# Attention and MLP block on one core: order of two VectorE reads in each attention slot, MLP factors in six pieces, and a rearranged opening

## The chip, the cores and the metric

The kernel runs on one NeuronCore of a Trainium2 chip. The metric is the device time of one execution in microseconds (us). The five engines are TensorE (PE, with its weight loads as PEld), VectorE (DVE), ScalarE (ACT), GpSimd (POOL) and SyncE (SP), which issues most of the DMAs. Each works through its own list of instructions in order and waits on semaphores.

## What is computed

The reference is one transformer block with 2048 rows of 576 values. Attention has 32 query heads of 128 on 16 key and value heads, over the last 512 entries of a cache; the MLP has 4608 hidden columns.

```python
mod = silu(c) @ w_mod                 # six vectors: sa, ca, ga, sb, cb, gb
h = layernorm(x) * (1 + ca) + sa
q = h @ wq                            # 32 heads of 128
p = softmax(q @ k.T * 128 ** -0.5)    # k, v: the last 512 rows, one pair for 2 query heads
x = x + ga * (concat(p @ v) @ wo)
h = layernorm(x) * (1 + cb) + sb
x = x + gb * ((silu(h @ w1) * (h @ w3)) @ w2)
```

## The kernel before

**Halves.** fp32 operands of a product are split into an fp16 high part and an fp16 remainder, the low part, after a scaling by a power of two. A product is then three products of halves: high by high, high by low, low by high. High parts are casts on ScalarE or GpSimd. Low parts are subtractions on GpSimd, or one instruction on VectorE.

**Slots and steps.** The rows are four blocks of 512 (`b`), each four tiles of 128 (`t`). Attention is a list of 128 slots `i`, one for each pair of a head and a block, and a slot has four steps `t` = 0 to 3, one for each row tile. The loop at L1564 writes out the order by hand, and each engine keeps it. Tasks that prepare later slots hang on a table: `at(i, t, task)` puts a task behind step `t` of slot `i`, and `step_at` counts steps of four to a slot. In step `t` of slot `i`:

- `scores(i, t)` (L475): three PE products into one of two banks `pss`. DVE takes the row maximum (L487) and makes the exponent's offset (L488).
- `weights` (L491): ACT's exponential `p` (L500) reads that bank and frees it. `half_high` and `half_low` split `p` on ACT and POOL, and a transposing DMA turns three of the four tiles. The fourth is turned on PE at `t` = 1 of the next slot: ACT casts it (L527), and DVE makes its low part (`turn_low`, L552, `ptw`) at `t` = 2.
- `query(i + 1, t)` (L410, L414): a part of the next slot's query product, for `t` < 3. ACT writes the high part of `qT` (L467), DVE the low part (L473).
- `attend_out` (L584): half of the product of one row tile with `wo`, six PE matmuls into the two banks `pe` (L433). There is one buffer `pe`. Every second call ends a tile, at `t` = 1 and at `t` = 3, and DVE then adds the tile into the accumulator (L592, `acc<-pe,factors,acc`). The next call's matmuls must wait until that read of `pe` is over.
- `normalize(i - 2)` (L567) at `t` = 1: DVE multiplies the value product `po` of an earlier slot with the softmax denominators `r`, which a DMA spreads over the partitions, into `on` (L571). `split_on` splits `on` at `t` = 3.
- At the end of a slot, `values(i - 1)` (L554): twelve PE products with `v` into `po` (L562). The third needs the low part of `ptw`, so L552.

Before the change the `normalize` call stands ahead of `attend_out` in step `t` = 1, right behind the score product.

**Opening.** Before slot 0, the first block goes through layernorm statistics on DVE (`norm_stats`, `bn_stats` and `bn_aggr`), modulation vectors, and `modulate_first`, which makes `h` of block 0 in halves. `put_in` splits a head's `wq` (`split_in`: two passes on ACT, then POOL's subtraction). `scale_first` finds one scale for the modulation vectors: a maximum, a small PE product, and a chain of small DVE instructions. Statistics of block 1 run on DVE behind `modulate_first`: two tiles ahead of slot 0's low part of `qT`, two behind it. `h` of block 1 is needed by the query product of slot 2, which is spread over slot 1. For each of its five column groups `m`, `make_h` has PE transpose four tiles into one of two banks `pt` (L240), DVE or ACT read the bank into `hf` (L249, L251), POOL cast that to the high part (L252) and POOL subtract for the low part (L254, L256). The values `v` of group 0 are peaked (`find`), scaled and split (L376 on ACT, L367 on DVE) by tasks in slots 0 and 1.

**MLP factors.** `act_factors` (L1180) makes a table of factors on DVE in five pieces, hung on five steps near the end of attention and, for the second half of the table, on five steps of the MLP.

Of the kernel before, what the change touches and what calls it, by code (L numbers as in the profile page):

```python
# [20 lines left out]
P = 128  # L21
# [27 lines left out]
def tile_block(  # L49
# [140 lines left out]
    def norm_stats(b, t):  # L190
# [4 lines left out]
            nc.vector.bn_stats(st[:, h, :], acc[b][:, t, h * HALF : (h + 1) * HALF])  # L195
        nc.vector.bn_aggr(norms[b][0][:, t, :], st.rearrange("p a b -> p (a b)"))

    def norm_root(b):
        rstd = norms[b][0][:, :, 1]
        nc.vector.tensor_scalar(rstd, rstd, EPS, None, op0=ALU.add)  # L200
        nc.scalar.activation(rstd, rstd, AF.Sqrt)

    def norm_scale(b):
# [15 lines left out]
    def norm_rows(b, t):  # L219

        mv, xn = norms[b]
        xt = pool.tile([P, D + DR], F32, tag="xn", name="xn", bufs=ST)
        if t < 2 or b not in shifts:
            nc.vector.tensor_scalar(
                xt[:, :D], acc[b][:, t, :], mv[:, t, 0:1], mv[:, t, 1:2], op0=ALU.subtract, op1=ALU.mult
            )
        else:
            nc.scalar.activation(
                xt[:, :D], acc[b][:, t, :], AF.Identity, bias=shifts[b][:, t : t + 1], scale=mv[:, t, 1:2]
            )  # L230
            if t == ST - 1:
                del shifts[b]
        nc.gpsimd.tensor_copy(xt[:, D:], xt[:, DC * P : D])
        xn[t] = xt

    def turn_rows(b, m, tag):

        ps = t_bank() if tag == "T" else bank(tag, "ps_n")
        for t in range(ST):
            nc.tensor.transpose(ps[:, t * P : (t + 1) * P], norms[b][1][t][:, m * P : (m + 1) * P], ident)  # L240
        return ps

    def modulate(hT, m, ps, shift, gain, on_vector=False):

        g, s = gain[:, m : m + 1], shift[:, m : m + 1]
        hf = pool.tile([P, SB], F32, tag="hf", name="hf", bufs=HF)
        high = hT[:, m if m < DC else 2 * DC, :]
        if on_vector:
            nc.vector.tensor_scalar(hf, ps, g, s, op0=ALU.mult, op1=ALU.add)  # L249
        else:  # L250
            nc.scalar.activation(hf, ps, AF.Identity, bias=s, scale=g)  # L251
        nc.gpsimd.tensor_copy(high, hf)  # L252
        if m < DC:
            nc.gpsimd.tensor_sub(hT[:, DC + m, :], hf, high)  # L254
        else:
            nc.gpsimd.tensor_sub(high[DR:], hf[DR:], high[DR:])  # L256

    def modulate_first(hT, turned, shift, gain):

        def make(m, h):  # L260
            g, s = gain[:, m : m + 1], shift[:, m : m + 1]
            if m % 2:
                nc.vector.tensor_scalar(h, turned[m], g, s, op0=ALU.mult, op1=ALU.add)
            else:
                nc.scalar.activation(h, turned[m], AF.Identity, bias=s, scale=g)

        for m in range(DC + 1):
            make(m, hT[:, m if m < DC else 2 * DC, :])
        for m in (DC, 1, 0, 3, 2):
            tag, bufs = ("p", PB) if m < DC else ("hf", HF)  # L270
            h = pool.tile([P, SB], F32, tag=tag, name="hf", bufs=bufs)
            make(m, h)
            if m < DC:
                (nc.vector if m % 2 else nc.gpsimd).tensor_sub(hT[:, DC + m, :], h, hT[:, m, :])
            else:
                nc.gpsimd.tensor_sub(hT[DR:, 2 * DC, :], h[DR:], hT[DR:, 2 * DC, :])

# [57 lines left out]
    def up_of(g, k):  # L335
        return peaks[g][:, 10 + k : 11 + k]

    def split_in(raw, g, j):

        w = pool.tile([P, 2, DC + 1, P], F16, tag="w", name="wq", bufs=WB)  # L340
        nc.scalar.activation(raw, raw, AF.Copy, scale=up_of(g, j))
        nc.scalar.copy(w[:, 0], raw)
        nc.gpsimd.tensor_sub(w[:, 1], raw, w[:, 0])
        return w

    def load_out(g):

# [735 lines left out]
    def scale_first(ps):  # L1083

        small = odd.tile([P, 16], F32, tag="us", name="us")
        nc.vector.tensor_scalar(mod_a[:, 1], mod_a[:, 1], 1.0, None, op0=ALU.add)
        nc.vector.tensor_reduce(small[:, 0:1], mod_a, axis=AX.XY, op=ALU.max, apply_absolute_value=True)
        spread = pool.tile([P, SB], F32, tag="kv", name="spread", bufs=8)
        nc.vector.tensor_scalar(spread[:, :P], ident, small[:, 0:1], None, op0=ALU.mult)
        nc.tensor.matmul(ps[:, :P], ones, spread[:, :P], start=True, stop=True)  # L1090
        nc.vector.tensor_reduce(small[:, 2:3], ps[:, :P], axis=AX.X, op=ALU.max)
        powers(small, small[:, 2:3], 0, 1, 5, 2.0**-9)
        nc.vector.tensor_scalar(mod_a, mod_a, small[:, 10:11], None, op0=ALU.mult)
        vecs["shift", "a"], vecs["gain", "a"] = mod_a[:, 0], mod_a[:, 1]
        nc.vector.tensor_scalar(score_down, small[:, 5:6], SCALE / Q_DOWN, None, op0=ALU.mult)

    def scale_gate(kind, small, to):

# [81 lines left out]
    def act_factors(lo, hi, piece):  # L1180

        top, h_down = mlp_small[:, 2:3], mlp_small[:, 5:6]
        both = stats.rearrange("p (g j) k -> p g j k", j=2)[:, lo:hi]
        downs, pairs = both[:, :, :, 0], both[:, :, :, 1]
        a = acts_down[:, lo:hi]
        if piece == 0:
            nc.vector.tensor_max(a, pairs[:, :, 0], pairs[:, :, 1])
            nc.vector.tensor_scalar(a, a, top, 2.5 * D * 2.0**-13.5, op0=ALU.mult, op1=ALU.mult)
        elif piece == 1:
            nc.vector.tensor_scalar(a, a, top, 2.0**-60, op0=ALU.mult, op1=ALU.max)  # L1190
            d = in_down[:, 2 * lo : 2 * hi]
            nc.vector.tensor_scalar(d, d, h_down, None, op0=ALU.mult)
        elif piece < 4:
            j = piece - 2
            nc.vector.reciprocal(pairs[:, :, j], a)
            nc.vector.tensor_mul(pairs[:, :, j], pairs[:, :, j], downs[:, :, j])
        else:
            if hi == G:
                hi += 1
                nc.vector.tensor_copy(acts_down[:, G : G + 1], acts_down[:, G - 1 : G])  # L1200
            d = out_down[:, lo:hi]
            nc.vector.tensor_scalar(d, d, mlp_gate_down, None, op0=ALU.mult)
            nc.vector.tensor_mul(d, d, acts_down[:, lo:hi])

    def find(into, u, k, *key):
# [56 lines left out]
    for u, (g, blocks, whole) in enumerate(uses):  # L1262
# [8 lines left out]
        if u:  # L1271
            A = dict(load=-22, keys=-17, wq=-13, total=-9, scale=-9, put=-8, turn=-5, vals=-1)
            if u == 1:
                A.update(load=-16, keys=-13, wq=-13)
            A = {k: R + v for k, v in A.items()}
            step_at(A["load"], load, keys, u, load_kv, k_cache, g)
            for j in range(2):
# [64 lines left out]
    for late in range(turns):  # L1342
# [15 lines left out]
            plan += [(step, make, number + k, maker, w, k), (step + STORE, store_now, number + k)]  # L1358
        for step, task, *args in plan:
            late_at(total + step, task, *args)  # L1360
    for piece in range(5):
        late_at(2 * len(ORDER) * turns + len(ORDER) + 1 + piece, act_factors, (NF - FEW) // 2, G, piece)
    for k, (i, t) in enumerate(((n - 4, 0), (n - 4, 2), (n - 3, 0), (n - 2, 0))):
        at(i, t, load_wset, 0, k)
# [36 lines left out]
    def begin_h(b):  # L1401
        hT[b] = new_h()

    def make_h(b, m, on_vector=False):
        modulate(hT[b], m, turn_rows(b, m, "T"), vecs["shift", "a"], vecs["gain", "a"], on_vector)

    def statistics(i, b, steps):
        for t in range(ST):
# [86 lines left out]
    at(109, 2, make_cols, "gain", "b", 4, 1.0, "T")  # L1495
    at(109, 3, lambda: spread_peaks("b", mlp_small))
    at(110, 1, lambda: scale_cols("b", t_bank(), mlp_small, 2.0**-8))
    for piece in range(5):
        step_at(ST * (n - 4) + 2 + piece, act_factors, 0, (NF - FEW) // 2, piece)
    for b in (2, 3):  # L1500
        for t in range(ST):
# [27 lines left out]
    warm(junk, WARM[0])  # L1529
    take_sums(0, 0, 3)  # L1530
    powers(peaks[0], peaks[0][:, 5:10], 0, 3, 5, 2.0**-14)
    put_in(0, 0)
    for m in (0, 1, 2, 3, 4):
        weigh_col(wms[1], 1, m, True)
    keys[0] = split_k(keys[0], 0)
    put_in(0, 1)
    scale_first(junk)
    warm(junk, WARM[1])
    begin_h(0)
    modulate_first(hT[0], turned, vecs["shift", "a"], vecs["gain", "a"])  # L1540
    score_factors(0)
    keys[0] = split_k_low(*keys[0], 0)
    for t in (0, 1):
        norm_stats(1, t)
    query(0, len(QP) - 1)
    for t in (2, 3):
        norm_stats(1, t)
    norm_root(1)
    at(0, 0, norm_scale, 1)
    at(0, 1, find, vals, 0, 3)  # L1550
    step_sum(3, totals, taken, 0, 3, 4)
    at(0, 3, find_scales, 0, 3, 4)
    at(1, -1, put_values, 0)
    at(1, 0, put_values_low, 0)
    for t in range(ST):
        at(0, t // 2, norm_rows, 1, t)
    at(0, 2, begin_h, 1)
    for m in range(DC + 1):
        at(*((0, 2), (0, 3), (1, -1), (1, 0), (1, 1))[m], make_h, 1, m, m % 2 == 1)
    for d, step in enumerate((5, 6, 7, 4, 5)):  # L1560
        step_at(step, weigh, 2, d)

# [1 line left out]
    for i in range(n + 2):  # L1564
        run(i, -1)
        for t in range(ST):
# [6 lines left out]
                turn(slot, tile)  # L1573
            if i < n:
                scores(i, t)
            if 2 <= i <= n and t == 1:
                normalize(i - 2)
            if 1 <= i <= n and t == 2:
                turn_low(i - 1, ST - 1)
                if i == n:  # L1580
# [20 lines left out]
                    next(stream)  # L1601
            for piece in outs.get((i, t), ()):
                attend_out(*piece, (i, ("total", t)))
            run(i, ("total", t))
            run(i, ("taken", t))
            run(i, t)
# [81 lines left out]
```

## Time and profile before

| | |
|---|---|
| median of 3 runs | 2758.36 us (2758.09 to 2758.54) |
| the profiled execution: time | 2758.39 us |
| the profiled execution: span in the trace | 2756.2 us |
| TensorE busy | 2685.1 us, 97% |
| VectorE, GpSimd, ScalarE busy | 72%, 68%, 59% |
| granted TensorE clock, mean | 0.995 |

The span reaches from the first to the last instruction of the trace; the execution's own time is 2.2 us longer. In the rows of a timeline the columns are start and duration in us, engine, line, operation, output<-inputs, shapes and count, and in brackets the idle time of that engine ahead of the row and what ended it. Rows of PE overlap by their pipeline's depth. In the rows of waits the three numbers are us in total, times, and the longest. Attention ends at about 1625 us; the rest is the MLP.

### The profile page before, as it was taken

How to read it: one execution, taken by the hardware profiler on the slowest of the kernel's cores; microseconds unless marked ns; L12 is line 12 of the kernel's file. 1: busy time of each engine (PE TensorE's matmuls, PEld its weight loads, DVE VectorE, ACT ScalarE, POOL GpSimd, SP SyncE). 2: the span in 40 equal slices, each digit the busy share in tenths (PEclk: the TensorE clock that was granted, in tenths of full speed). 3: DMA queues.
4: the chain of work that ended last, by engine and by line, in shares of the span. 5: the costliest groups of instructions: out<-in, count | busy, mean ns of one | idle time of the engine just before them, and what ended most of it. 6: DMA issues, size and time to landing. Idle time of an engine off the chain costs nothing. (4 is left out here: it accounts for less than half of the span.)

```text
span 2756.2 us, 44751 instructions
## 1 busy us (share of the span) xinstructions
PE 2685.1 (97%) x15406; PEld 1512.8 (55%) x15406; DVE 1997.3 (72%) x3555; ACT 1617.8 (59%) x3013; POOL 1881.1 (68%) x1748
## 2 busy tenths in 40 slices
PE   6899999999999999999999999999999999999998
PEld 3455555555555555555555555555555555555555
DVE  7877788877788787877876667777766656666666
ACT  5777778777777877777677735544443333333332
POOL 5577788888788977877669637688873465333435
PEclk8999999999999999999999999999999999999999
DMA  5778888778786887989889945656643444333332
GB/s 186 171 178 193 194 182 188 175 176 189 169 185 166 190 196 180 214 181 210 192 189 208 256 131 171 200 167 200 210 149 108 161 121 128 103 102 111 104 107 87
DMA packets 593460, 463.84 MB, mean 168 GB/s; under 512 B 442704, under 2 KB 472528, under 8 KB 592208
## 3 DMA queue, kind: packets, MB, share of 16 engines
q1 hardware_dynamic: 592944, 460.69, 65.5%
q8 instruction: 121, 1.98, 0.3%
q14 instruction: 107, 0.88, 0.1%
q10 hardware_dynamic: 288, 0.30, 0.0%
HBM read 264.19 MB, written 95.99 MB: 131 GB/s over the span
## 5 line engine op out<-in xcount | busy, mean ns | idle before, releaser
L537 POOL TENSOR_TENSOR hp<-p,hp 128x512 f16<-128x512 f32 x384 | 449.6, 1173 | 266.3 <-ACT hp L532 143.8
L500 ACT ACTIVATE p<-pss,table,factors 128x512 f32<-128x512 f32 x512 | 396.9, 775 | 354.9 <-DVE table L488 182.5
L849 PEld LDWEIGHTS <-wset 128*128 128x128 f16 x3528 | 344.5, 98 | 337.4 <-issue 4.4
L487 DVE TENSOR_REDUCE table<-pss 128x1 f32<-128x512 f32 x512 | 350.5, 685 | 206.0 <-PE pss L483 202.0
L849 PE MATMUL py<-hset,wset 128*128 128x512 f16 x2016 | 483.1, 380 | 0.0
L433 PE MATMUL pe<-o 128*128 128x288 f16 x3024 | 453.1, 286 | 10.1 <-DVE acc L592 9.6
L483 PE MATMUL pss<-k,qT 128*128 128x512 f16 x1536 | 418.8, 380 | 14.2 <-ACT p L500 10.4
L433 PEld LDWEIGHTS <-o 128*128 128x128 f16 x3072 | 300.5, 98 | 184.5 <-issue 15.7
L562 PE MATMUL po<-ptw,v 128*128 128x512 f16 x1536 | 358.2, 381 | 8.2 <-DMA ptw<-hp 4.1
L849 PE MATMUL px<-hset,wset 128*128 128x512 f16 x1512 | 361.5, 379 | 1.6 <-ACT p L500 1.6
L94 POOL TENSOR_TENSOR akv<-u,akv 128x512 f16<-128x512 f32 x141 | 165.0, 1180 | 179.2 <-ACT akv L93 171.4
L410 PE MATMUL pq<-hT,wq 128*128 128x512 f16 x1092 | 282.3, 381 | 1.8 <-POOL hT L252 1.1
L532 ACT CAST hp<-p 128x512 f16<-128x512 f32 x384 | 237.3, 618 | 13.2 <-POOL hT L256 0.6
L562 PEld LDWEIGHTS <-v 128*128 128x128 f16 x1536 | 147.8, 98 | 172.8 <-issue 16.2
L483 PEld LDWEIGHTS <-qT 128*128 128x128 f16 x1536 | 147.8, 98 | 129.2 <-issue 15.5
L934 PEld LDWEIGHTS <-akv 128*128 128x128 f16 x1728 | 169.0, 98 | 89.3 <-issue 0.8
L592 DVE SCALAR_TENSOR_TENSOR acc<-pe,factors,acc 128x576 f32<-128x576 f32 x252 | 204.6, 812 | 4.3 <-PE pe L433 4.3
L582 POOL TENSOR_TENSOR o<-on,o 128x512 f16<-128x512 f32 x128 | 150.3, 1174 | 54.0 <-ACT o L581 51.9
L410 PEld LDWEIGHTS <-wq 128*128 128x128 f16 x1092 | 107.2, 98 | 128.5 <-issue 2.9
L928 DVE SCALAR_TENSOR_TENSOR acc<-pf,table,acc 128x576 f32<-128x576 f32 x140 | 113.5, 811 | 80.8 <-PE pf L934 80.8
L1027 ACT COPY u<-py 128x512 f32<-128x512 f32 x72 | 42.2, 586 | 202.1 <-PE py L849 200.2
L1020 ACT ACTIVATE s<-s,table 128x512 f32<-128x512 f32 x72 | 52.0, 722 | 176.3 <-DVE s L1019 176.3
(246 smaller groups left out, 4793.8 us busy)
## 6 DMA issues: line engine op xcount, KB each, us to landing
wset<-wd SPq DMA_DIRECT2D x213, 320.0 KB, 3.2
r<-row SPq DMA_DIRECT2D x128, 256.0 KB, 3.9
oset<-od SPq DMA_DIRECT2D x106, 288.0 KB, 3.2
wraw<-in_w SPq DMA_DIRECT2D x36, 768.0 KB, 5.4
wd<-wmade SPq DMA_DIRECT2D x75, 320.0 KB, 3.3
wset<-wd SPq DMA_DIRECT2D x71, 160.0 KB, 2.2
w2raw<-in_w SPq DMA_DIRECT2D x19, 576.0 KB, 5.2
wd<-ring SPq DMA_DIRECT2D x33, 320.0 KB, 2.9
```

The source lines that it names most:

```text
L94: eng.tensor_sub(halves[:, 1], src, halves[:, 0])
L410: nc.tensor.matmul(ps, w[:, k // 2, m, :], hT[:, DC + m if k == 1 else m, :], start=s == 0, stop=False)
L433: nc.tensor.matmul(ps[:, h, :HALF], o[:, x, rows], w[:, y, h * HALF : (h + 1) * HALF], start=first and n == 0, stop=last and n == 2,)
L483: nc.tensor.matmul(pss, q[:, x, rows], k[:, y, :], start=n == 0, stop=n == 2)
L487: nc.vector.tensor_reduce(nm[:, 0:1], pss, axis=AX.X, op=ALU.max, negate=True)
L500: nc.scalar.activation(p, pss, AF.Exp, bias=nm[:, 1:2], scale=factor, accum_out=st["l"][:, t : t + 1])
L532: nc.scalar.copy(hp[:, 0, :], state[i]["p", t])
L537: nc.gpsimd.tensor_sub(hp[:, 1, :], state[i].pop(("p", t)), hp[:, 0, :])
L562: nc.tensor.matmul(po, v[:, x, c, :], pt[:, y, c, :], start=c == 0 and n == 0, stop=c == KC - 1 and n == 2)
L592: nc.vector.scalar_tensor_tensor(a, ps[:, :, :HALF], factors[:, uses[u][0], 2:3], a, op0=ALU.mult, op1=ALU.add)
L849: nc.tensor.matmul(ps, w[:, a, :], h[:, b, :], start=start and n == 0, stop=stop and n == 6, skip_group_check=True)
L934: nc.tensor.matmul(ps[:, h, :HALF], a[:, rows], w[:, b, :], start=m == 0, stop=m == 2)
```

## The change

1. In the slot loop, `normalize(i - 2)` moves from behind the score product to behind `attend_out` in the same step `t` = 1.
2. `act_factors` has six pieces: the last of the five had two instructions, and the second of them is a piece of its own, one step later.
3. The opening. Of block 1's statistics, three tiles become sums on ScalarE (`norm_sums`: a pass with `Copy` that accumulates the negated mean, and one with `Square` around it), three of these six passes ahead of `modulate_first` and three behind it. The fourth tile keeps `bn_stats` on VectorE, within `scale_first`, where VectorE waits for the small product; GpSimd brings it to the form of the others, and makes `score_down`. The subtractions of `split_in` follow behind that on GpSimd. `modulate_first` gives one of GpSimd's two subtractions to VectorE. For block 1, `modulate` writes the high part of `h` from the bank itself: for `m` = 0 on VectorE, for the others on ScalarE, with `hf` always on VectorE, and only the subtraction is left to GpSimd. The tasks around it move: the columns `m` = 2 to 4 come earlier, the peak of group 0's values and all that hangs on it later (scales from slot 0 step 3 to slot 1 step 1, `v` from slot 1 steps -1 and 0 to step 2), and for group 1 the peaks of keys, values and `wq` one step later.

```diff
-            if 2 <= i <= n and t == 1:
-                normalize(i - 2)
...
             for piece in outs.get((i, t), ()):
                 attend_out(*piece, (i, ("total", t)))
+            if 2 <= i <= n and t == 1:
+                normalize(i - 2)
...
+    def norm_sums(b, t, squares):
...
+        if squares:
+            nc.scalar.activation(o, a, AF.Square, bias=mv[:, t, 0:1], accum_out=mv[:, t, 1:2])
+        else:
+            nc.scalar.activation(o, a, AF.Copy, scale=-1.0 / D, accum_out=mv[:, t, 0:1])
...
-        if on_vector:
+        if early:
             nc.vector.tensor_scalar(hf, ps, g, s, op0=ALU.mult, op1=ALU.add)
+            if not m:
+                nc.vector.tensor_scalar(high, ps, g, s, op0=ALU.mult, op1=ALU.add)
+            else:
+                nc.scalar.activation(high, ps, AF.Identity, bias=s, scale=g)
         else:
             nc.scalar.activation(hf, ps, AF.Identity, bias=s, scale=g)
-        nc.gpsimd.tensor_copy(high, hf)
+            nc.gpsimd.tensor_copy(high, hf)
...
-                (nc.vector if m % 2 else nc.gpsimd).tensor_sub(hT[:, DC + m, :], h, hT[:, m, :])
+                (nc.vector if m else nc.gpsimd).tensor_sub(hT[:, DC + m, :], h, hT[:, m, :])
...
-        else:
+        elif piece == 4:
...
+        else:
+            hi += hi == G
+            d = out_down[:, lo:hi]
             nc.vector.tensor_mul(d, d, acts_down[:, lo:hi])
...
-                A.update(load=-16, keys=-13, wq=-13)
+                A.update(load=-16, keys=-12, wq=-12)
...
+    for k in range(3):
+        norm_sums(1, *divmod(k, 2))
     scale_first(junk)
+    for j in range(2):
+        split_in_low(wqs[0, j], raws[j])
...
-    for t in (0, 1):
-        norm_stats(1, t)
+    for k in range(3, 6):
+        norm_sums(1, *divmod(k, 2))
     query(0, len(QP) - 1)
-    for t in (2, 3):
-        norm_stats(1, t)
     norm_root(1)
     at(0, 0, norm_scale, 1)
-    at(0, 1, find, vals, 0, 3)
-    step_sum(3, totals, taken, 0, 3, 4)
-    at(0, 3, find_scales, 0, 3, 4)
-    at(1, -1, put_values, 0)
-    at(1, 0, put_values_low, 0)
+    at(0, 3, find, vals, 0, 3)
+    step_sum(5, totals, taken, 0, 3, 4)
+    at(1, 1, find_scales, 0, 3, 4)
+    at(1, 2, put_values, 0)
+    at(1, 2, put_values_low, 0)
...
-        at(*((0, 2), (0, 3), (1, -1), (1, 0), (1, 1))[m], make_h, 1, m, m % 2 == 1)
+        at(*((0, 2), (0, 3), (0, 3), (1, -1), (1, 0))[m], make_h, 1, m, True)
```

**VectorE in an attention slot.** These are VectorE's rows of before from step `t` = 1 of one slot (its score maximum, L487) to the low part `ptw` of step 2.

```order
L487 TENSOR_REDUCE table<-pss 128x1
L488 TENSOR_SCALAR table<-table,factors 128x1
L571 TENSOR_TENSOR on<-po,r 128x512
L592 SCALAR_TENSOR_TENSOR acc_92<-pe,factors,acc_92 128x576
L305 TENSOR_REDUCE top<-kvraw 128x1
L1162 TENSOR_REDUCE peak_cols<-w2raw 128x1
L487 TENSOR_REDUCE table<-pss 128x1
L488 TENSOR_SCALAR table<-table,factors 128x1
L552 TENSOR_TENSOR ptw<-pt,ptw 128x4x128
```

The same stretch of the changed kernel, whose line numbers are 25 to 29 higher there (L512 is L487, L596 is L571, L617 is L592, L577 is L552):

```order
L512 TENSOR_REDUCE table<-pss 128x1
L513 TENSOR_SCALAR table<-table,factors 128x1
L617 SCALAR_TENSOR_TENSOR acc_92<-pe,factors,acc_92 128x576
L596 TENSOR_TENSOR on<-po,r 128x512
L326 TENSOR_REDUCE top<-kvraw 128x1
L1191 TENSOR_REDUCE peak_cols<-w2raw 128x1
L512 TENSOR_REDUCE table<-pss 128x1
L513 TENSOR_SCALAR table<-table,factors 128x1
L577 TENSOR_TENSOR ptw<-pt,ptw 128x4x128
```

Only the two rows behind the first maximum have changed places, and everything from the peaks to `ptw` stands behind both of them as before.

**ScalarE in slots 0 and 1.** These are ScalarE's rows of before from the last exponential of slot 0 (`p_530`) to the high part of slot 2's `qT`; `v_550` is the high part of group 0's values, `hf_557` and `hf_627` are columns of block 1's `h`, `wm2` and `wmr` belong to a modulation vector.

```order
L500 ACTIVATE p_530,l_443<-pss_523,table_223,factors_101 128x512
L376 ACTIVATE v_550<-kvraw_246,us_319 128x512
L251 ACTIVATE hf_557<-pt_552,mod_a_93 128x512
L500 ACTIVATE p_569,l_568<-pss_562,table_223,factors_101 128x512
L532 CAST hp_571<-p_569 128x512
L156 ACTIVATE wm2_248<-wm2_248,sc_80 128x576
L500 ACTIVATE p_603,l_568<-pss_597,table_223,factors_101 128x512
...
L527 CAST ptw_491<-pt_592 128x4x128
L251 ACTIVATE hf_627<-pt_622,mod_a_93 128x512
L156 ACTIVATE wmr_225<-wmr_225,sc_80 64x576
L500 ACTIVATE p_643,l_568<-pss_636,table_223,factors_101 128x512
...
L467 ACTIVATE qT_652<-pq_575 128x512
```

The changed kernel's rows from the same exponential (now `p_526`) to `v` (now `v_648`), with `hT_508` the high part of block 1's `h`:

```order
L525 ACTIVATE p_526,l_440<-pss_519,table_223,factors_101 128x512
L270 ACTIVATE hT_508<-pt_529,mod_a_93 128x512
L270 ACTIVATE hT_508<-pt_538,mod_a_93 128x512
L270 ACTIVATE hT_508<-pt_547,mod_a_93 128x512
L525 ACTIVATE p_564,l_563<-pss_557,table_223,factors_101 128x512
...
L270 ACTIVATE hT_508<-pt_580,mod_a_93 128x512
L156 ACTIVATE wm2_248<-wm2_248,sc_80 128x576
L525 ACTIVATE p_601,l_563<-pss_595,table_223,factors_101 128x512
...
L156 ACTIVATE wmr_225<-wmr_225,sc_80 64x576
L525 ACTIVATE p_635,l_563<-pss_628,table_223,factors_101 128x512
...
L492 ACTIVATE qT_644<-pq_570 128x512
L401 ACTIVATE v_648<-kvraw_246,us_319 128x512
```

The high part of `v` has moved from right behind slot 0's last exponential to behind slot 2's `qT`, and four reads of `pt` that write `hT` stand where two reads that wrote `hf` stood. (The casts `hp`, and in this list one `ptw`, are left out at the dots.)

More of the change, by code (lines that the diff above doesn't have):

```diff
@@ L196, in norm_stats @@
         nc.vector.bn_aggr(norms[b][0][:, t, :], st.rearrange("p a b -> p (a b)"))
+    def norm_sums(b, t, squares):
+        if not t and not squares:
+            norms[b] = odd.tile([P, ST, 2], F32, tag="mv", name="mv"), {}
+            norms["out", b] = pool.tile([P, D + DR], F32, tag="xn", name="xn", bufs=ST)
+        mv, o, a = norms[b][0], norms["out", b][:, :D], acc[b][:, t, :]
+        if squares:
+            nc.scalar.activation(o, a, AF.Square, bias=mv[:, t, 0:1], accum_out=mv[:, t, 1:2])
+        else:
+            nc.scalar.activation(o, a, AF.Copy, scale=-1.0 / D, accum_out=mv[:, t, 0:1])
     def norm_root(b):
         rstd = norms[b][0][:, :, 1]
-        nc.vector.tensor_scalar(rstd, rstd, EPS, None, op0=ALU.add)
+        if ("out", b) in norms:
+            nc.vector.tensor_scalar(rstd, rstd, 1.0 / D, EPS, op0=ALU.mult, op1=ALU.add)
+        else:
+            nc.vector.tensor_scalar(rstd, rstd, EPS, None, op0=ALU.add)
         nc.scalar.activation(rstd, rstd, AF.Sqrt)
@@ L224, in norm_rows @@
             nc.vector.tensor_scalar(
-                xt[:, :D], acc[b][:, t, :], mv[:, t, 0:1], mv[:, t, 1:2], op0=ALU.subtract, op1=ALU.mult
+                xt[:, :D], acc[b][:, t, :], mv[:, t, 0:1], mv[:, t, 1:2],
+                op0=ALU.add if ("out", b) in norms else ALU.subtract, op1=ALU.mult,
             )
@@ L233, in norm_rows @@
         nc.gpsimd.tensor_copy(xt[:, D:], xt[:, DC * P : D])
+        if t == ST - 1:
+            norms.pop(("out", b), None)
         xn[t] = xt
@@ L241, in turn_rows, with modulate @@
         return ps
-    def modulate(hT, m, ps, shift, gain, on_vector=False):
+    def modulate(hT, m, ps, shift, gain, early=False):
         g, s = gain[:, m : m + 1], shift[:, m : m + 1]
@@ L336, in up_of, with split_in @@
         return peaks[g][:, 10 + k : 11 + k]
-    def split_in(raw, g, j):
+    def split_in(raw, g, j, low=True):
         w = pool.tile([P, 2, DC + 1, P], F16, tag="w", name="wq", bufs=WB)
@@ L342, in split_in, with split_in_low @@
         nc.scalar.copy(w[:, 0], raw)
+        if low:
+            split_in_low(w, raw)
+        return w
+    def split_in_low(w, raw):
         nc.gpsimd.tensor_sub(w[:, 1], raw, w[:, 0])
-        return w
     def load_out(g):
@@ L1090, in scale_first @@
         nc.tensor.matmul(ps[:, :P], ones, spread[:, :P], start=True, stop=True)
+        norm_stats(1, ST - 1)
         nc.vector.tensor_reduce(small[:, 2:3], ps[:, :P], axis=AX.X, op=ALU.max)
+        for k, by in ((0, -1.0), (1, float(D))):
+            last = norms[1][0][:, ST - 1, k : k + 1]
+            nc.gpsimd.tensor_scalar(last, last, by, None, op0=ALU.mult)
         powers(small, small[:, 2:3], 0, 1, 5, 2.0**-9)
@@ L1094, in scale_first @@
         vecs["shift", "a"], vecs["gain", "a"] = mod_a[:, 0], mod_a[:, 1]
-        nc.vector.tensor_scalar(score_down, small[:, 5:6], SCALE / Q_DOWN, None, op0=ALU.mult)
+        nc.gpsimd.tensor_scalar(score_down, small[:, 5:6], SCALE / Q_DOWN, None, op0=ALU.mult)
     def scale_gate(kind, small, to):
@@ L1202, in act_factors @@
             nc.vector.tensor_scalar(d, d, mlp_gate_down, None, op0=ALU.mult)
+        else:
+            hi += hi == G
+            d = out_down[:, lo:hi]
             nc.vector.tensor_mul(d, d, acts_down[:, lo:hi])
@@ L1360, in tile_block @@
             late_at(total + step, task, *args)
-    for piece in range(5):
+    for piece in range(6):
         late_at(2 * len(ORDER) * turns + len(ORDER) + 1 + piece, act_factors, (NF - FEW) // 2, G, piece)
@@ L1402, in begin_h, with make_h @@
         hT[b] = new_h()
-    def make_h(b, m, on_vector=False):
-        modulate(hT[b], m, turn_rows(b, m, "T"), vecs["shift", "a"], vecs["gain", "a"], on_vector)
+    def make_h(b, m, early=False):
+        modulate(hT[b], m, turn_rows(b, m, "T"), vecs["shift", "a"], vecs["gain", "a"], early)
     def statistics(i, b, steps):
@@ L1497, in tile_block @@
     at(110, 1, lambda: scale_cols("b", t_bank(), mlp_small, 2.0**-8))
-    for piece in range(5):
+    for piece in range(6):
         step_at(ST * (n - 4) + 2 + piece, act_factors, 0, (NF - FEW) // 2, piece)
@@ L1531, in tile_block @@
     powers(peaks[0], peaks[0][:, 5:10], 0, 3, 5, 2.0**-14)
-    put_in(0, 0)
+    raws = [wqs[0, j] for j in range(2)]
+    wqs[0, 0] = split_in(raws[0], 0, 0, False)
     for m in (0, 1, 2, 3, 4):
@@ L1535, in tile_block @@
     keys[0] = split_k(keys[0], 0)
-    put_in(0, 1)
+    wqs[0, 1] = split_in(raws[1], 0, 1, False)
+    for k in range(3):
+        norm_sums(1, *divmod(k, 2))
     scale_first(junk)
+    for j in range(2):
+        split_in_low(wqs[0, j], raws[j])
     warm(junk, WARM[1])
```

## Prediction

> **What bounds the kernel now.** I read the page first, then the waits of PE, then the groups of DVE, then the timeline of single slots, then that of the first 65 us. The page names the bound.
>
> ```profile
> span 2756.2 us, 44751 instructions
> ...
> PE 2685.1 (97%) x15406; PEld 1512.8 (55%) x15406; DVE 1997.3 (72%) x3555; ACT 1617.8 (59%) x3013; POOL 1881.1 (68%) x1748
> ...
> PE   6899999999999999999999999999999999999998
> ```
>
> PE is idle for only 2756.2 − 2685.1 = 71.1 us. The change removes no work from PE, so it can only move these 71 us: by the digits, the most in the first two slices of 69 us, the rest thinly spread. The profiled execution took 2758.4 us, 2.2 more than its span and equal to the median to 0.03, so sums on the span carry over. About 0.2%, or 5.5 us, is what a measurement of this kernel can tell from no change.
>
> PE's waits say which stalls the edits touch. The numbers are us in total, times and longest:
>
> ```profile
> PE pss L483 <- ACT p L500: 10.4, 15, 2.5
> PE pe L433 <- DVE acc L592: 9.6, 10, 2.4
> ...
> PE po L562 <- DVE ptw L552: 3.2, 7, 0.7
> PE pq L414 <- POOL hT L256: 2.9, 1, 2.9
> ```
>
> The second row is what the moved `normalize` aims at: PE waits until DVE has read `pe`, 9.6 us in ten places. The third is what comes behind both of DVE's instructions: the low part `ptw` that the value product needs.
>
> **Part 1: `normalize` behind the accumulator.** A slot at 390 us shows the usual state, DVE first, then PE:
>
> ```profile
> 389.01 1.08 DVE L571 TENSOR_TENSOR on<-po,r 128x512 f32<-128x512 f32 x1
> 390.00 0.82 DVE L592 SCALAR_TENSOR_TENSOR acc<-pe,factors,acc 128x576 f32<-128x576 f32 x1
> ...
> 392.58 0.69 DVE L487 TENSOR_REDUCE table<-pss 128x1 f32<-128x512 f32 x1
> ...
> 393.43 0.68 DVE L552 TENSOR_TENSOR ptw<-pt,ptw 128x512 f16<-128x512 f32 x1
> ```
>
> ```profile
> 389.03 0.90 PE L433 MATMUL pe<-o 128*128 128x288 f16 x6
> ...
> 393.42 0.59 PE L562 MATMUL po<-ptw,v 128*128 128x512 f16 x2
> 394.17 1.02 PE L562 MATMUL po<-ptw,v 128*128 128x512 f16 x4 [0.15 <-DVE ptw L552]
> ```
>
> `on` runs while PE makes the tile's second half (389.03 to 389.93), and the accumulator read starts 0.07 us after PE's end. It can't start sooner in another order: DVE would now idle for that 0.99 us, start the read at the same 390.00, and run `on` behind it. Everything behind it on DVE (two peaks, the next maximum, `ptw`) comes up to 0.95 us later. In my arithmetic over 123 slots of attention this holds in 106.
>
> *What it saves.* Where `on` starts late, it holds the read:
>
> ```profile
> 581.83 1.06 DVE L571 TENSOR_TENSOR on<-po,r 128x512 f32<-128x512 f32 x1 [2.94 <-DMA r<-row]
> 582.80 0.81 DVE L592 SCALAR_TENSOR_TENSOR acc<-pe,factors,acc 128x576 f32<-128x576 f32 x1
> ```
>
> ```profile
> 583.67 0.90 PE L433 MATMUL pe<-o 128*128 128x288 f16 x6 [2.43 <-DVE acc L592]
> ```
>
> Here DVE waited 2.94 us for `r`, and PE lost 2.43. All ten waits of the 9.6 us have such a late `on` ahead of them. With the read in front, PE's wait goes, but where `r` is late DVE still stands behind the read and gains no more than the read's own 0.81; part of the loss then returns at the next thing that PE wants of DVE. Taking 0.81 off the time that comes back late, slot by slot, I keep 7.1 of the 9.6 (bounds 0.81 × 10 = 8.1 and, if half returns, 4.8).
>
> *What it costs.* The cover is PE's lead at `po`: the third of its matmuls needs `ptw`. At the first and the last of the places where that cover is too thin:
>
> ```profile
> 111.92 0.68 DVE L552 TENSOR_TENSOR ptw<-pt,ptw 128x512 f16<-128x512 f32 x1
> ...
> 112.07 1.18 PE L562 MATMUL po<-ptw,v 128*128 128x512 f16 x4
> ```
>
> ```profile
> 1426.89 1.45 PE L562 MATMUL po<-ptw,v 128*128 128x512 f16 x6 [0.55 <-DVE ptw L552]
> ```
>
> At 112 the third matmul starts at 112.07 + 0.43 = 112.50 and `ptw` ends at 112.60: a start 0.1 ahead of the modelled end is no wait, so there is no slack, and the delay becomes a wait. For each slot I took 0.95, less DVE's idle gaps between the read and `ptw`, less that slack. Thirty slots come out with a new wait, 12.3 us in sum. Eleven of them, the first and last above and the slot at 390 among them, are of half a microsecond or more and make 8.8; nineteen small ones make 3.5. A mean of 0.18 is near the 0.1 by which such starts are known, so I count half of it. Cost: 8.8 + 1.7 = 10.5 (bounds 0, if PE meets another wait ahead of `po` in these slots, and 13.3 with one more wait of 1.0 at a late `qT`).
>
> Every new wait is one of up to 0.95 us. How the clock takes that:
>
> ```profile
> 580.00:590.00 10.00, 7.43 (x41) 3.75 (x40) 7.40 (x13) 5.15 (x11) 6.07 (x7) 1.00 0.91 166
> ```
>
> With a wait of 2.43 us in it (and 0.14 more elsewhere), this window of 10 us keeps a granted clock of 1.00 (the number ahead of the DMA share). So I add nothing for the clock here. The Trainium skill ("TensorE: Matmul & The Clock Gate", Part 1) has the clock fall to half after an idle window of about 3.4 us; by it the sum of part 1 would be the same, and the trace agrees at 2.43 us, but it bears on part 3.
>
> **Part 2: the sixth piece.** The multiplication that moves to the next step is of this kind:
>
> ```profile
> 1546.34 1.17 DVE L1187 TENSOR_TENSOR table<-table 128x14 f32<-128x14 f32 x1
> ```
>
> One such instruction, twice in the kernel, starts a step later on an engine that is 72% busy; it is hidden by DVE's idle time. I take 0, with a gain of at most 1.17 if it stood ahead of a read that PE waits for.
>
> **Part 3: the opening.** Rows of PE, DVE and ACT on which the chain rests:
>
> ```profile
> 32.74 0.60 ACT L467 ACTIVATE qT<-pe 128x512 f16<-128x512 f32 x1 [3.10 <-PE pe L423]
> ...
> 33.72 0.77 DVE L195 BATCH_NORM_STATS2 bst<-acc 128x6 f32<-128x288 f32 x2
> ...
> 34.64 0.64 DVE L473 SCALAR_TENSOR_TENSOR qT<-pe,qT 128x512 f16<-128x512 f32 x1
> ...
> 35.34 0.39 PE L483 MATMUL pss<-k,qT 128*128 128x512 f16 x1 [1.33 <-DVE qT L473]
> ```
>
> ```profile
> 46.12 1.12 PE L240 MATMUL pt<-ident,xn 128*128 128x128 f32 x4 [2.09 <-ACT hf L251]
> ...
> 50.67 0.38 PE L410 MATMUL pq<-hT,wq 128*128 128x512 f16 x1 [0.75 <-POOL hT L254]
> ...
> 54.59 0.38 PE L410 MATMUL pq<-hT,wq 128*128 128x512 f16 x1 [1.07 <-POOL hT L252]
> ...
> 59.42 0.75 PE L414 MATMUL pq<-hT,wq 128*128 128x512 f16 x2 [2.94 <-POOL hT L256]
> ...
> 61.31 3.64 PE L562 MATMUL po<-ptw,v 128*128 128x512 f16 x12
> ```
>
> ```profile
> 48.61 0.76 ACT L251 ACTIVATE hf<-pt,mod_a 128x512 f32<-128x512 f32 x1
> ...
> 57.06 0.78 ACT L500 ACTIVATE p<-pss,table,factors 128x512 f32<-128x512 f32 x1
> ...
> 58.01 0.62 ACT L532 CAST hp<-p 128x512 f16<-128x512 f32 x1
> ...
> 60.20 0.60 ACT L467 ACTIVATE qT<-pq 128x512 f16<-128x512 f32 x1 [1.58 <-PE pq L414]
> ```
>
> - *The first `qT`.* DVE loses its two statistics pairs ahead of the low part, which ends about 1.5 us earlier (33.1 for 34.64); PE's wait of 1.33 at 35.34 goes. The passes on ACT lie in the 3.10 us that it waits for PE at 32.74. Gain 1.5, if it lasts.
> - *The transposes.* For block 1 a bank `pt` is now read twice, by DVE into `hf` and by ACT into `hT`, and order shows ACT's read waiting for DVE's. The ACT form takes 0.76, the same instruction on DVE I estimate at 0.8. PE's wait of 2.09 at 46.12 thus stays, and begins earlier: I get PE idle from about 42.9 to 46.0, and the 1.5 is spent. The Trainium skill ("PSUM — Partial Sum Buffer", the section on bank collisions) says that two engines may not be on one bank at once, reads included; no row here shows two engines reading a bank, and if both could read together, 0.76 for each of two banks, 1.5 us, would stay.
> - *Slot 1's query product.* POOL's cast goes, so the three waits 0.75 + 1.07 + 2.94 = 4.8 us vanish, and PE reaches the end of slot 2's query at about 54.4 for 60.1.
> - *`v`.* The value product at 61.31 is what comes next, and `v` is now written behind slot 2's `qT` on ACT: after the exponential and cast at 57.06 and 58.01, both pulled ahead with PE. I get the high part at about 57.7 and `po` from 58.45, for 61.31: 2.9 us earlier. PE idles for about 3.4 us ahead of it. At full pace such a matmul adds (1.45 − 1.02) / 2 = 0.215 us (six at 1426.89, four at 394.17), so the twelve at 61.31, in 3.64, lost 0.9 to a low clock already. At half pace I count ten of them at twice 0.215: 2.15 lost, 1.25 more than before, and 0.4 for the low part of `v`, which DVE makes behind the high part: 1.6 in all. By the skill's 3.4 us such a fall would just be reached; without it 2.1 more would stay.
>
> Net gain 2.9 − 1.6 = 1.3 us. Bounds: 6.5 if `v` isn't late (60.1 − 54.4 = 5.7 for the query product, and half of the 1.5), and a loss of 3 if `v`, behind more tasks on ACT, comes only where `po` did before, at half pace.
>
> **Sum.** 2758.4 − 7.1 + 10.5 + 0 − 1.3 = 2760.5 us: no change that can be told.
>
> **Rivals.**
> - *The new waits don't bind* (faster). PE comes to `po` later in those slots, since scores also wait for ACT (10.4 us of waits on `p`), or DVE has caught up; the 7.1 stays. For it: before, only 7 slots show a wait for `ptw`, 3.2 us. Against: in the slot at 390 there is no gap on DVE. 2758.4 − 7.1 − 1.3 = 2750.0, to 2748 if PE's clock doesn't fall ahead of `po` in the opening.
> - *The new waits bind in full and carry over* (slower). DVE ends the slot late, and its next maximum and the exponential start late: in nine more slots the delay isn't made up by the slot's end, 6.2 us, and 1.0 at `qT`. 2758.4 − 7.1 + 12.3 + 7.2 − 1.3 = 2769.5. It decides where DVE has less than 0.95 us of idle between the read and the next slot's first maximum. Against: at 388 to 394 DVE is full, but it is 72% busy over the span.
> - *The opening keeps what it gains.* `v` isn't the bound, and 6.5 stays: 2758.4 − 7.1 + 10.5 − 6.5 = 2755.3. Against: order puts `v` behind slot 2's `qT`.
>
> **How the numbers follow.** The forecast has 0.38 (its own range 2756 to 2765, from the half-counted small waits and the opening's bounds), the first rival 0.27, the second 0.20, the third 0.15. The range from 2748 to 2770 holds the forecast, the first and third whole, and the second to about its middle. Faster by over 0.2% (below 2752.9): 0.25 of the first and 0.07 of the third, 0.32. Slower (above 2763.9): 0.20 of the second and 0.08 of the forecast, 0.28. Between: 0.40.
>
> **What would show it.** In the changed profile the wait of `pe` for `acc` should fall from 9.6 to under 2 us, and that of `po` for `ptw` rise from 3.2 to about 14; `po` of slot 0 should start near 58.5 with an idle of PE ahead of it. If `po` waits for `ptw` less than 6 us, part 1's cost is wrong and the first rival holds; if `pss` waits for `p` by over 15 us, the second; if `po` of slot 0 starts before 56, the third.

## The result and the profile after

The changed kernel takes 2781.14 us (median of 6 runs, 2779.13 to 2783.47), the one before 2758.45 (6 runs) on the same chips. The ratio of the means is 1.0077, with a 95% interval of 1.0064 to 1.0090. By the medians it is 22.7 us slower, outside the predicted range (2748 to 2770).

The page of the changed kernel, for its profiled execution of 2781.09 us:

```profile
span 2779.0 us, 44813 instructions
...
PE 2691.9 (97%) x15406; PEld 1511.3 (54%) x15406; DVE 1998.7 (72%) x3550; ACT 1623.0 (58%) x3026; POOL 1871.9 (67%) x1745
```

PE's idle time is 2779.0 − 2691.9 = 87.1 us, for 71.1 before. PE also counts 6.8 us more as busy for the same 15406 matmuls. The two make the 22.8 us by which the span grew. The rows of PE's waits:

```profile
PE pss L508 <- ACT p L525: 12.9, 16, 2.6
PE po L587 <- DVE ptw L577: 12.7, 22, 1.8
...
PE pe L458 <- DVE table L1170: 5.8, 14, 0.5
PE pe L458 <- DVE us L336: 5.5, 12, 0.5
...
PE pe L458 <- DVE table L1199: 2.2, 5, 0.5
```

The wait of `pe` for `acc` is gone, but for 0.9 us on another matrix. The wait for `ptw` has risen from 3.2 us to 12.7, near the 14 that was forecast. The last three rows are new but for one wait of 0.2 us: PE waits for `pe` until DVE has made a small copy out of it (three lines of the kernel make such copies), 13.5 us in 31 places.

Where the time went is read best from when PE starts the first score product behind each value product, in the two traces. The first block is before, the second after; in each the first row is from the end of the opening, the second from near the end of attention:

```profile
114.81 0.38 PE L483 MATMUL pss<-k,qT 128*128 128x512 f16 x1
...
1561.35 0.59 PE L483 MATMUL pss<-k,qT 128*128 128x512 f16 x2
```

```profile
112.25 0.59 PE L508 MATMUL pss<-k,qT 128*128 128x512 f16 x2
...
1583.65 0.38 PE L508 MATMUL pss<-k,qT 128*128 128x512 f16 x1
```

I call the difference of such a pair of starts the drift. It is −2.6 us at the end of the opening and +22.3 near the end of attention, so attention lost 24.9; what follows added only 0.5. Between those rows the drift's steps upward, from slot to slot, make 36.0 us and its steps downward 11.1. Of 116 slots from 140 to 1535 us, 13 had DVE waiting ahead of `on` before the change: there the drift fell by 6.6 us. The other 103 lost 32.1.

A slot that lost 1 us shows both kinds of new wait, DVE first:

```profile
234.60 0.82 DVE L617 SCALAR_TENSOR_TENSOR acc<-pe,factors,acc 128x576 f32<-128x576 f32 x1 [0.90 <-PE pe L1164]
235.33 1.07 DVE L596 TENSOR_TENSOR on<-po,r 128x512 f32<-128x512 f32 x1
236.32 0.15 DVE L1170 COPY table<-pe 128x2 f32<-128x2 f32 x1
...
239.06 0.68 DVE L577 TENSOR_TENSOR ptw<-pt,ptw 128x512 f16<-128x512 f32 x1
```

```profile
235.50 0.59 PE L439 MATMUL pq<-hT,w 128*128 128x512 f16 x2
236.53 0.90 PE L458 MATMUL pe<-o 128*128 128x288 f16 x6 [0.44 <-DVE table L1170]
...
239.80 1.02 PE L587 MATMUL po<-ptw,v 128*128 128x512 f16 x4 [0.53 <-DVE ptw L577]
```

DVE idles 0.90 us ahead of the read, as forecast. Behind `on` stands a copy of 0.15 us, which takes the result of a peak's small product out of the bank `pe`. `attend_out` of step 2 must not write that bank before it, so PE waits 0.44 us; then it waits 0.53 for `ptw`. Together that is 0.97.

The waits of DVE from 100 to 1600 us, of before and then of after, show the price on DVE's side:

```profile
DVE table L487 <- PE pss L483: 200.4, 184, 2.3
...
DVE acc L592 <- PE pe L433: 3.0, 1, 3.0
```

```profile
DVE table L512 <- PE pss L508: 143.4, 131, 2.8
DVE acc L617 <- PE pe L458: 69.4, 83, 0.9
...
DVE acc L617 <- PE pe L1164: 11.8, 13, 0.9
DVE acc L617 <- PE pe L331: 11.8, 13, 0.9
DVE acc L617 <- PE pe L1196: 2.7, 3, 0.9
```

DVE's idle time ahead of the read has grown from 3.0 to 95.7 us, in 112 places of at most 0.9. Its wait for the scores has shrunk by 57 us. So more than half of the new idle time was taken from old idle time, and the question is where the rest went.

### The profile page after: what moved, and what is told of

Its sections match the earlier page's. It is cut to its first block, busy times and chain, and to the rows that moved or that the text cites. A ratio compares the mean times of both kernels' runs of the same rounds, so it can differ in the third digit from the quotient of the medians.

```text
span 2779.0 us, 44813 instructions
## 1 busy us (share of the span) xinstructions
PE 2691.9 (97%) x15406; PEld 1511.3 (54%) x15406; DVE 1998.7 (72%) x3550; ACT 1623.0 (58%) x3026; POOL 1871.9 (67%) x1745
## 5 line engine op out<-in xcount | busy, mean ns | idle before, releaser
L512 DVE TENSOR_REDUCE table<-pss 128x1 f32<-128x512 f32 x512 | 349.7, 683 | 148.6 <-PE pss L508 147.4
L508 PE MATMUL pss<-k,qT 128*128 128x512 f16 x1536 | 417.2, 379 | 15.4 <-ACT p L525 12.9
L587 PE MATMUL po<-ptw,v 128*128 128x512 f16 x1536 | 363.8, 382 | 20.5 <-DVE ptw L577 12.7
L617 DVE SCALAR_TENSOR_TENSOR acc<-pe,factors,acc 128x576 f32<-128x576 f32 x252 | 204.8, 813 | 101.8 <-PE pe L458 75.0
```

What stands on the lines that cost most here:

```text
L508: nc.tensor.matmul(pss, q[:, x, rows], k[:, y, :], start=n == 0, stop=n == 2)
L512: nc.vector.tensor_reduce(nm[:, 0:1], pss, axis=AX.X, op=ALU.max, negate=True)
L587: nc.tensor.matmul(po, v[:, x, c, :], pt[:, y, c, :], start=c == 0 and n == 0, stop=c == KC - 1 and n == 2)
L617: nc.vector.scalar_tensor_tensor(a, ps[:, :, :HALF], factors[:, uses[u][0], 2:3], a, op0=ALU.mult, op1=ALU.add)
```

## The experiments

In the diffs, − is the kernel named first. Medians stand beside the kernel before on the same chip, which took 2758.05 us for the first four, 2757.75 for the next four and 2760.83 for the last four.

**The parts alone.** The move in the kernel before; the opening with `normalize` in its old place and five pieces; the same with six pieces.

```diff
 # e1: before
-            if 2 <= i <= n and t == 1:
-                normalize(i - 2)
...
                 attend_out(*piece, (i, ("total", t)))
+            if 2 <= i <= n and t == 1:
+                normalize(i - 2)
```

> Before, with only normalize moved behind attend_out. Theory (the move alone costs it: the small copies out of the bank pe and the low part ptw come 0.95 us later behind the multiplication): slots 4 to 127 lose what they lost in the changed kernel, 25.4 us, and the opening is as before, so about 2784 us (2781 to 2787), with some 30 waits of pe for table or us (13 us) and 12 us of po for ptw. Rival (the opening's earlier start shifts transfers and tasks against each other, and that costs the most): under 2772.

Measured: 2788.27 us, ratio 1.0106 (1.0092 to 1.0120). Its drift ends at +23.9, with 34.9 us upward and 10.8 downward, 12.9 us of `po` for `ptw` and 13.7 of `pe` for the copies. That is 1.3 us above the theory's range; the trace is of the fastest of the four runs, 2782.61 us. The move alone makes the loss; the rival falls.

> The changed kernel with normalize back in its old place and the factors in five pieces, so the opening alone. Theory: the lead of 3.1 us at slot 4 lasts to the end, 2755.3 us (2754 to 2757). Rival (the opening shifts later slots and costs there): 2762 or more.

Measured: 2756.67 us, ratio 0.9995 (0.9986 to 1.0004). Its drift is −2.65 at slot 4 and −2.28 at the end of attention: the opening's gain is there and lasts through attention in the trace. Over the whole span this execution is only 0.1 us shorter than before (2756.1 for 2756.2), since its MLP took 2.2 longer, for a reason that isn't settled. The median is within the theory's range, and the difference is too small for the interval.

> The changed kernel with normalize back in its old place, six pieces kept. Theory: the sixth piece is worth nothing, so equal to the opening alone within 1 us, about 2755. Rival (the piece matters): a gain or loss of over 1.2 us against that run.

Measured: 2753.99 us, ratio 0.9986 (0.9977 to 0.9995), 2.7 under the opening alone, with overlapping intervals. By the number this is the rival's case, a difference of over 1.2. The trace has one difference that I put down to the piece, a wait for an MLP accumulation. With five pieces (e2), then with six (e4):

```profile
PE pe L959 <- DVE acc L953: 3.7, 2, 2.3
```

```profile
PE pe L959 <- DVE acc L953: 2.6, 2, 1.4
```

In all traces of kernels with six pieces this total is 2.6, and in the three with five it is 3.7 to 3.9. So the piece is worth about 1.1 us there. The rest of the 2.7 isn't settled.

**The copies ahead of the multiplication.**

```diff
 # e3: the changed kernel
-            if 2 <= i <= n and t == 1:
-                normalize(i - 2)
             run(i, ("total", t))
             run(i, ("taken", t))
+            if 2 <= i <= n and t == 1:
+                normalize(i - 2)
```

> The changed kernel with normalize one place later still, behind the small copies out of pe (take_sums, in_taken, out_taken). Theory: the 31 waits of pe for those copies, 13.5 us and about 0.15 more each for the broken pipeline, go, 18 us: about 2763 us (2760 to 2766); the 12.7 us of po for ptw stay. Rival (the copies are only where DVE's lateness shows, and PE meets it at the next wait anyway): 2775 or more.

Measured: 2777.43 us, ratio 1.0068 (1.0056 to 1.0081). The waits for the copies are gone, and yet only 3.7 us of the median with them. The intervals of the two kernels overlap, but the drift near the end of attention agrees: 19.0 us for 22.3. The theory that the copies are the main cost falls. The waits of e3:

```profile
PE po L587 <- DVE ptw L577: 19.8, 30, 1.8
PE pss L508 <- ACT p L525: 15.4, 20, 2.6
```

Much of what PE no longer waited for the copies it waited for `ptw` and the exponential. Only in ten slots, with a copy and enough idle time on DVE, did the loss of 0.6 us each simply go (6.0 us to 0.0).

**More cover ahead of `ptw`.** All products with the high part come first, in three kernels.

```diff
 # e5: the kernel of e3; e6: the changed kernel; e7: the kernel of e4
-        for c in range(KC):
-            for n, (x, y) in enumerate(((0, 0), (1, 0), (0, 1))):
+        parts = [(x, 0, c) for c in range(KC) for x in range(2)] + [(0, 1, c) for c in range(KC)]
+        for n, (x, y, c) in enumerate(parts):
...
```

> The kernel with the copies first (2777.4 us), and the value product in another order: all eight matmuls with the high part of ptw ahead of the four with the low part, so that PE's cover ahead of ptw grows from two matmuls (0.43 us) to eight (1.7 us). Theory (the lateness of 0.95 us is paid where PE first needs something from behind on, and with the copies moved that is ptw): the 19.8 us of po for ptw in 30 places, and 0.15 more for each broken pipeline, go, 24 us: about 2753 us (2750 to 2758). Rival (DVE's lateness is met at whatever PE wants next, the exponential, qT or the next slot's maximum, as it was when the copies were moved): 2768 or more.

> The changed kernel with the same order in the value product. Theory: the 12.7 us of po for ptw in 22 places go, with their broken pipelines 16 us, the 13.5 us of pe for the copies stay: about 2765 us (2762 to 2769). Rival (it is met elsewhere): 2775 or more.

> The control: normalize in its old place (2754.0 us), with the same order in the value product. Theory: only the 2.4 us of po for ptw in 6 places are there to be saved: 2751 us (2749 to 2754). If this order is worth more by itself, the two other runs must be read against this one.

Measured: 2768.73 us (ratio 1.0038, 1.0025 to 1.0051), 2774.61 (1.0055, 1.0043 to 1.0068) and 2747.59 (0.9960, 0.9947 to 0.9973). Against their own bases these are 8.7, 6.5 and 6.4 us less: within the noise, the order of products is worth as much without the move as with it. In e5 no wait for `ptw` is left among the large ones, but the first row of the waits is now this, for 15.4 in e3:

```profile
PE pss L508 <- ACT p L525: 21.0, 32, 2.6
```

So the rival of e5 holds; e6 ends far above its theory and 0.4 us short of its rival. With the waits for the copies and for `ptw` both out of the way, e5 is still 21.1 us above e7, the same kernel without the move. DVE's lateness is paid at whatever PE wants next, and no single taker is the cause.

The control was worth more than the 2.4 us of visible waits. A part of the reason is seen in the value product of one slot, in e4 and then in e7:

```profile
237.16 3.05 PE L587 MATMUL po<-ptw,v 128*128 128x512 f16 x12
```

```profile
237.21 2.75 PE L587 MATMUL po<-ptw,v 128*128 128x512 f16 x12
```

The same twelve matmuls take 0.30 us less. In e4 the third would start at 237.16 + 0.43 = 237.59, and `ptw` ends at 237.84: this short wait shows no idle time and only makes the row longer. Over 120 slots, from 115 to 1560 us, the rows of the value products make 334.7 us in e4 and 330.3 in e7, so 4.4 us less, of which 1.7 was visible idle time. The rest of the 6.4 isn't settled.

**The move where it pays.**

```diff
 # e8: the kernel of e4
-            if 2 <= i <= n and t == 1:
+            if 2 <= i <= n and t == 1 and i not in LATE:
                 normalize(i - 2)
...
                 attend_out(*piece, (i, ("total", t)))
+            if 2 <= i <= n and t == 1 and i in LATE:
+                normalize(i - 2)
...
+    LATE = (6, 36, 37, 44, 68, 69, 76, 84, 121, 124, 127)
```

> The kernel with normalize in its old place (2754.0 us), with the move in eleven slots alone: those in which its profile shows PE waiting for the accumulator (11.2 us in 11 places). Theory: the move pays where the multiplication is late, as the falls of 11 us in the drift of the changed kernel say: about 2745 us (2742 to 2748). Rival (the saving comes back as a later wait in these slots too): 2752 or more.

Measured: 2749.74 us, ratio 0.9970 (0.9959 to 0.9982), 4.3 us under e4, with overlapping intervals. The 11.2 us of `pe` for `acc` fell to 0.9, and `po` for `ptw` rose from 2.4 to 4.6. The drift, against e4's, falls by 6.5 us in the 13 slots with a late `on` and rises by 2.8 in the 103 others. So the move pays in its slots, with less than the theory's 9, and a part comes back: the answer lies between theory and rival.

**The multiplication later still.**

```diff
 # e9: the changed kernel
                 turn_low(i - 1, ST - 1)
+                if i >= 2:
+                    normalize(i - 2)
...
-            if 2 <= i <= n and t == 1:
-                normalize(i - 2)
```

> The changed kernel with normalize another step later, behind turn_low of step 2, so that accumulator read, copies, peaks and ptw all stand ahead of it. Theory A (what counts is DVE's own time: in step 1 it now idles 0.9 us for PE's second half, 96 us in 112 slots, and where DVE has little other idle time in the slot this is lost wherever the multiplication stands): 2765 to 2778 us. Theory B (what counts is what stands behind the multiplication, the copies and ptw, and neither is late here): 2755 us or less.

Measured: 2797.11 us, ratio 1.0138 (1.0122 to 1.0153). This is above both, and doesn't tell A from B, since it met a third wait: the next value product can't start before `on` has read the older one. DVE, then PE:

```profile
411.09 1.07 DVE L596 TENSOR_TENSOR on<-po,r 128x512 f32<-128x512 f32 x1
```

```profile
412.22 2.76 PE L587 MATMUL po<-ptw,v 128*128 128x512 f16 x12 [0.44 <-DVE on L596]
```

Such waits make 28.1 us in 37 places. Another 36.4 in 45 places are put down to a cast on ACT, but in 44 of them PE begins 0.06 to 0.10 us after the end of `on` as well (0.06 in the row above), so these are most likely the same wait.

**Filling or removing DVE's gap.**

```diff
 # e10: the changed kernel
+            for piece in outs.get((i, t), ()) if t == 1 else ():
+                attend_out(*piece, (i, ("total", t)))
             if i + 1 < n and t < ST - 1:
                 query(i + 1, t)
...
-            for piece in outs.get((i, t), ()):
+            for piece in outs.get((i, t), ()) if t != 1 else ():
                 attend_out(*piece, (i, ("total", t)))
 # e11: the changed kernel
+            if t == 1:
+                early = [k for k in tasks.get((i, t), ()) if k[0] in (find, in_peak) and k[1][0] is not wos]
+                for k in early[:1]:
+                    tasks[i, t].remove(k)
+                    k[0](*k[1])
             for piece in outs.get((i, t), ()):
```

> The changed kernel with PE's order altered in step 1: attend_out ahead of the query product, so that PE's second half is done when DVE has its maximum, and DVE need not idle ahead of the read; normalize stays behind the read. Theory A: the loss of 36 us in the drift goes and the saving of 11 stays, so about 2745 us (2742 to 2752), unless PE now waits for o at the earlier place. Theory B: copies and ptw still stand behind the multiplication, but it ends 0.9 us sooner, so the same. Rival to both (the query part or the scores of step 2 come late instead): 2765 or more.

Measured: 2749.15 us, ratio 0.9958 (0.9946 to 0.9971). In the slot that the prediction showed, the read now follows DVE's maximum at once, and `on` stands behind it all the same:

```profile
382.74 0.21 DVE L513 TENSOR_SCALAR table<-table,factors 128x1 f32<-128x1 f32 x1
382.87 0.81 DVE L617 SCALAR_TENSOR_TENSOR acc<-pe,factors,acc 128x576 f32<-128x576 f32 x1
383.59 1.09 DVE L596 TENSOR_TENSOR on<-po,r 128x512 f32<-128x512 f32 x1
```

DVE's idle time ahead of the read falls from 95.7 us to 7.1. The drift's steps upward fall from 36.0 to 4.7, and its falls stay, at 11.4. In the 103 slots without a late `on`, the loss of 32.1 us falls to 0.2. So with almost no idle time ahead of the read, the multiplication behind it cost next to nothing. A and B had both forecast this, so e10 doesn't tell them apart; and no run has this order of PE with the multiplication in front, so what PE's order is worth by itself is not known. In the opening e10 also gains 1.7 us more than the changed kernel: its row for 112.25 starts at 110.51.

> The changed kernel with the first short peak of step 1 (0.7 to 0.95 us, in some 35 slots) put ahead of the accumulator read, into DVE's idle time; normalize stays behind the read, copies behind both. Theory A: the slots with such a peak lost 13 us, which go: about 2769 us (2766 to 2774). Theory B: the copies are as late as before, only ptw comes sooner: 2776 or more.

Measured: 2769.19 us, ratio 1.0033 (1.0020 to 1.0045), as A forecast. The slot with two peaks, with one of them in the gap:

```profile
390.51 0.68 DVE L326 TENSOR_REDUCE top<-kvraw 128x1 bf16<-128x512 f32 x1
391.47 0.82 DVE L617 SCALAR_TENSOR_TENSOR acc<-pe,factors,acc 128x576 f32<-128x576 f32 x1 [0.28 <-PE pe L458]
392.20 1.08 DVE L596 TENSOR_TENSOR on<-po,r 128x512 f32<-128x512 f32 x1
```

It lost 0.97 us in the changed kernel and 0.37 here. In 26 slots with such a peak and no late `on` the loss falls from 10.1 to 4.4 us, though copies and `ptw` still stand behind `on`. Six of them keep 0.6 each, and in all six PE waits 0.44 to 0.46 for a copy: there B's taker still sets the price. In the 77 others the loss goes from 22.0 to 17.2. Of these, the 18 slots right behind one with such a peak fall from 5.2 to 2.1, one slot near the end of attention from 2.1 to 0.4 (a wait for the exponential), and the 58 that the edit doesn't touch stay, at 14.7 and 14.6.

**The two gains together.** The diffs of e8 and e7 in one kernel.

> The move in the eleven slots alone (2749.7 us), with all high products of the value product first (worth 6.4 us in the control). If the two gains add: 2743 us (2740 to 2746).

Measured: 2745.64 us, ratio 0.9947 (0.9934 to 0.9959). The gains add within the noise. This is the lowest ratio of the study, with e10 (0.9958) and e7 (0.9960) behind it, whose intervals overlap with its own.

## Why the prediction was wrong

- **What `normalize` behind the read does to DVE: right.** The read starts 0.9 us after DVE could have, in 112 places, and everything behind comes up to 0.95 later.
- **The savings: 7.1 forecast, near.** In 13 slots with a late `on` the drift fell by 6.6 us. Tried alone in eleven slots, eight of which are among these 13, the move gave 4.3.
- **The cost: 10.5 forecast, 32.1 measured in 103 slots. This is the step that failed**: "The cover is PE's lead at `po`: the third of its matmuls needs `ptw`." It took one taker for the only one. That taker's own wait was sized well: `po` for `ptw` came to 12.7 us, for about 14 forecast. Three things were left out. The copies out of `pe`: they stand between `on` and the peaks, in the same bank that `attend_out` writes next; the slot I had looked at has none. The other takers: e3 and e5 removed the copies' and `ptw`'s waits in turn, and most of the time came back at the next one. And the hidden part, 6.8 us more of PE's busy time: PE shows 109 idle gaps of over 0.15 us for 68 before, and each new one also costs the 0.16 us or so by which two rows of PE otherwise overlap (41 × 0.16 = 6.6, an estimate); short waits inside a row are in it too.
- **What sets most of the cost instead** is DVE's own idle time within the slot. Of the 103 slots, 53 had less than 2.5 us of it before, from this read to the next slot's, and lost 24.6 us; 50 had more and lost 7.5. This is a tendency, with a boundary drawn afterwards. The ten slots with only a copy, in both groups, make 6.0 of these: there the copy alone sets the price. The runs say more: with `on` still behind the read, e10, which gave DVE's time back nearly everywhere, took the loss of the 103 slots to 0.2 us, and e11, which gave it back in some slots, took it to 21.6, with the fall in those slots and the ones right behind them. That DVE is only 72% busy over the span, which I held against the second rival, says nothing of these slots.
- **The rivals.** The first and the third did not come. The third's sign did: `po` of slot 0 starts at 55.61, before 56. But the drift at slot 4 is −2.6, not the rival's −6.5. The second, that the lateness carries over to DVE's next maximum, comes nearest to what happened, and had 0.20. Its price of 2769.5 still lacked the copies. Its sign in the profile, `pss` waiting for `p` over 15 us, did not come (12.9). In e3, without the waits for the copies, it was 15.4, so they probably held PE first.
- **The opening: −1.3 forecast, −2.6 in the drift.** That this is so near is partly luck, since two errors go against each other. `po` of slot 0 started 5.7 us earlier than before, for 2.9 forecast. Of these, 2.0 were lost by the next score product (61.06 for 64.78), for 1.6 forecast, and 1.1 more by slot 4, which the forecast didn't have. The fall of the clock came. The rows of PE, then three stretches with the length, the busy time of PE and the other engines, and the granted clock as the third number from the end; the last of them is of the trace before:

```profile
54.42 0.16 PE L331 MATMUL pe<-top,peak_cols 128*128 128x4 bf16 x1 [2.10 <-DVE top L326]
55.61 0.61 PE L587 MATMUL po<-ptw,v 128*128 128x512 f16 x1 [1.02 <-ACT v L401]
56.40 4.87 PE L587 MATMUL po<-ptw,v 128*128 128x512 f16 x11 [0.18 <-DVE v L392]
```

```profile
51.10:54.40 3.30, 1.23 (x6) 0.47 (x5) 3.09 (x6) 3.14 (x8) 2.42 (x2) 1.00 0.00 0
54.50:61.30 6.80, 5.59 (x14) 1.89 (x14) 4.38 (x11) 1.93 (x4) 1.15 (x1) 0.50 0.81 181
...
967.70:971.00 3.30, 3.30 (x14) 1.64 (x13) 2.53 (x7) 2.30 (x5) 0.69 (x1) 0.50 1.53 146
```

  Eleven matmuls take 4.87 us, 0.44 each, for 0.215 at full pace. The granted clock is 1.00 up to 54.40 and 0.50 from 54.50 on, so it fell behind the idle time of 2.10 us alone, before the 1.02 us. The Trainium skill ("TensorE: Matmul & The Clock Gate", Part 1) puts the fall at an idle window of about 3.4 us; here 2.10 us were enough. The length of one idle time doesn't settle it: in the trace before, 2.43 us of it ahead of 583.67 left the clock at 1.00, as the prediction read, but behind 2.01 us ahead of 966.32 it was 0.50 from 967.7 to 971.0. So a wait of 2 us can bring a fall, and part 1's zero for the clock was not safe. The loss in attention isn't made by it: the mean granted clock from 115 to 1561 us is 1.00 in both traces. The wait of the third transposes stayed too, at 2.92 us for 2.09, behind ACT's read of the bank.
- **The sixth piece: 0 forecast, with a bound of 1.17.** It came out near the bound, 1.1.

## What to carry to other kernels

An instruction that runs while its engine would otherwise wait costs that engine its length when it is moved out of there: here the wait stayed as idle time (95.7 us in 112 places), and the work had to find room later in the same slot or make PE wait. Ask of the engine's idle time slot by slot, not over the span, and list everything behind the moved instruction that any engine takes, down to copies of 0.15 us that hold a shared bank. If the read must come first, first make what it waits for come earlier, as e10 does on PE.

## What the runs showed that was not expected

- Waits that show no idle time: the same row of twelve matmuls took 3.05 us where `ptw` was late and 2.75 where it wasn't. Reordering the products gave 6.4 us, where the rows of waits named 2.4.
- Removing a wait of 13.5 us in 31 places gave 3.7 us. A row of waits is no price list: the next taker stands behind each.
- The value product had a third claim on `on`: with `on` about 2 us later (e9), the bank of the older product made at least 28.1 us of waits in 37 places.
